# Attention weights of a pair turned by one transfer instead of two, with a new plan of loads and units

## The chip, the cores and the metric

The kernel runs on one core of a Trainium2 chip. The metric is the device time of one execution in microseconds (us). Engines are named as the profile names them: PE multiplies matrices (PEld is its weight load), DVE, ACT and POOL work on vectors, SP issues transfers (DMA). PE and its products write to banks of an accumulator memory; the other data lie in a memory of 128 partitions.

## The reference

Two stages follow each other. The first is attention with a decay, over 8 batches of 8 heads, 576 positions and 64 numbers per head:

```
scores = q @ k^T / 8 + cum[:, None] - cum[None, :]     # cum: running sum of log(clip(f)) of this head
scores = -1e9 where key > query                        # causal
attn   = softmax(scores); x = attn @ v
```

The second takes the 4608 rows of x (8 heads x 64 = 512 numbers each) through a gated block: g = x @ w_gate, out = (g * sigmoid(g) * (x @ w_val)) @ w_out, with 1536 inner columns. All inputs and the output are float32.

## The kernel before, in words

**Units.** Two heads make a pair (32 pairs, p = 0 to 31, four to a batch). The 576 queries of a head are cut in 9 blocks of 64, and a block of both heads of a pair fills 128 partitions. The blocks come in two groups: group 0 has blocks 0 to 3, group 1 blocks 4 to 8 (HI and LO, lines 224 and 225). A unit is a pair and a group.

**One pair.** k and q are loaded (load_pair, L385), cast to bf16 (prepare, L410 to L414), turned on PE into a bank named tx (L428) and copied out as kt and qz (L440, L442); qz takes two copies, one for each head. The running sums of log f of all heads are made once at the start (L342 to L345), written to DRAM (L354) and loaded per pair as cb, spread over partitions (L394); pair 0 gets its cb through a product with a matrix of ones instead (select, L369, and copies L373). scores makes products q by k into banks named sp, of which there are two (L461, and L465 for the causal mask), DVE adds cb and keeps the row's extreme (L477: t, tm), ACT takes the exponential with the row's sum (L491: e or eo). normalize adds a guard to the sums and inverts them (L505 to L509: lr), then POOL, or ACT for pairs under 8, scales e to bf16 weights (L526, L524) in a buffer pk, in slices of 128 keys by 128 queries: 6 slices for group 0, 19 for group 1 (NSL, line 226).

**Turning the weights.** The product with v needs the slices with keys on partitions. For pairs 0 to 7 (ON_PE, line 230) PE turns each slice with the identity matrix (L550) into a bank, and DVE or ACT copies it to a buffer pT (L555). For pairs 8 to 31 a transposing transfer on SP's queue writes pT from pk (L538), one for each group. There are two pk and two pT buffers for each group. weighted multiplies pT by v (L576, into a tx bank, 4 products for group 0 and 10 for group 1), spread copies the result into xT (L600), a ring of 2560 columns. BOTH (line 237) is the pair from which the two groups are weighted in one operation of 14 products; below it each group has its own.

**The second stage.** The rows go in tiles of 256, 256, seven of 512, 256, 128 and 128 (TILES). gate makes the products with w_gate and w_val (L657, both into banks gv, from x of all four pairs of the batches in question), ACT takes tanh (L663), two DVE operations make hh (L665, L668); project multiplies by w_out (L685), halves (L692, L694) and stores (L696). The weights are loaded by POOL's queue in column blocks with a cast (L632, L636): wg0 and wv0 are columns 0 to 255, wg2 and wv2 256 to 511, and so on. v is loaded in five pieces for a batch (L615) and cast (L619).

**What sets the order.** The code writes no order for the engines by hand. Every step is an Op with its engines and an estimated length, reads, writes, a priority and, for transfers, a wire time. Plan.order (from L59) is a list scheduler: again and again it takes the operation that can start first by these estimates (ties by priority), gives it an engine and a buffer, and so fixes each engine's order; the engines then run in that order and wait on semaphores. SPARE is a handicap, in ns, for ACT and DVE on casts and scalings; MOST bounds how many gv banks turned weights (p), output (o) and gate products (f) may hold; SOON, BACK and CBACK say how early loads of a pair may go; SLACK bears on which line of a shared pool goes first. STARTUP (line 244) is the order of the first loads: p is k and q of a pair, f9 the log f input, c a pair's cb, v a piece of v, w a block of weights. A load waits until the one AHEAD places ahead of it has landed, a weight load on POOL also for the one BEHIND places ahead. HEAD (line 245) is the order of the first eight units: group 0 of pairs 0 to 3, then group 1 of pairs 1, 0, 3, 2.

The functions that the diff touches:

Of the kernel before, what the change touches and what calls it, by code (L numbers as in the profile page):

```python
# [9 lines left out]
BF16 = mybir.dt.bfloat16  # L10
# [21 lines left out]
class Plan:  # L32
# [6 lines left out]
    def __init__(self):  # L39
        self.slack = 0  # L40
        self.ops, self.pools, self.home, self.where, self.turn, self.banks = [], {}, {}, {}, {}, set()
        self.line, self.most = {}, {}

    def pool(self, name, bufs):
        self.pools[name] = bufs

    def key(self, key, pool, turn=None, line=None):

        self.home[key], self.turn[key], self.line[key] = pool, turn, line

    def buf(self, key):
        return self.pools[self.home[key]][self.where[key]]
# [6 lines left out]
    def order(self):  # L59
        writers, users = {}, {}  # L60
        for o in self.ops:
            for k in o.writes:
                writers.setdefault(k, []).append(o)
            for k in {*o.writes, *o.reads, *o.holds}:
                users.setdefault(k, []).append(o)
        waiting, kids = {}, {}
        for o in self.ops:
            deps = {d.n: d for k in o.reads for d in writers[k] if d is not o}
            deps.update((d.n, d) for d in o.after)
            o.deps = list(deps.values())  # L70
# [12 lines left out]
        lines = {}  # L83
        for name, x in turn:
            lines.setdefault(name, []).append((name, x))
        left = {k: len(v) for k, v in users.items()}
        until = {k: 0 for k in users}
        slots = {name: [None] * len(b) for name, b in self.pools.items()}
        free = {e: 700 for e in ("PE", "DVE", "ACT", "POOL", "SP")}
        wire = {True: 0, False: 0}  # L90
        ready = {o.n: 0 for o in self.ops if not waiting[o.n]}
        done, using = [], {}

        def room(o, now=None):

            at, take = 0, []
            for k in o.writes:
                if k not in self.home or k in self.where:
                    continue
                name, best = self.home[k], None  # L100
                x = name, self.line[k]
                mine = sum(x == (self.home[y], self.line[y]) for y, _ in take)
                if turn[x][taken[x] + mine] != k:
                    return None
                if x in self.most:
                    held = sum(y is not None and left[y] > 0 and self.line[y] == x[1] for y in slots[name])
                    if held + mine >= self.most[x]:
                        return None
                for n, held in enumerate(slots[name]):
                    if any(n == b and name == self.home[x] for x, b in take):  # L110
                        continue
                    t = 0 if held is None else until[held] if not left[held] else None
                    if t is not None and (best is None or t < best[0]):
                        best = (t, n)
                if best is None:
                    return None
                at = max(at, best[0])
                take.append((k, best[1]))
            if now is not None:
                for k, _ in take:  # L120
                    for x in lines[self.home[k]]:
                        if x[1] != self.line[k] and taken[x] < len(turn[x]):
                            y = turn[x][taken[x]]
                            q = opener[y]
                            if rank(y) < rank(k) and q.n in ready and ready[q.n] <= max(now, at) + self.slack and room(q) is not None:
                                return None
            return at, take

        while ready:
            best = None  # L130
            for n, r in ready.items():
                o = self.ops[n]
                got = room(o, r)
                if got is None:
                    continue
                for e, dur in o.engs.items():
                    s = max(r, got[0], free[e])
                    for k in o.reads:
                        if k in using and using[k][0] != e:
                            s = max(s, using[k][1])  # L140
                    c = (s + o.bias.get(e, 0), o.prio, n, e, dur, got[1])
                    if best is None or c[:4] < best[:4]:
                        best = c
            if best is None:
                raise RuntimeError("no operation can start: " + ", ".join(str(self.ops[n].writes) for n in list(ready)[:20]))
            s, _, n, e, dur, take = best
            o = self.ops[n]
            s -= o.bias.get(e, 0)
            if e == "PE" and s < COLD:
                dur *= 2  # L150
            for k, b in take:
                name = self.home[k]
                self.where[k] = b
                slots[name][b] = k
                taken[name, self.line[k]] += 1
            o.start, o.eng = s, e
            free[e] = s + dur
            for k in o.reads:
                if self.home.get(k) in self.banks:
                    using[k] = e, s + dur + 30  # L160
            if o.dma:
                q = e == "POOL"
                at = max(wire[q], s + (2550 if q else 2000))
                both = max(0, min(2 * o.dma, wire[not q] - at))
                wire[q] = at + o.dma + both / 2
                wire[not q] += both / 2
                if o.ring:
                    free[e] = max(free[e], wire[q] - 1450)
                o.end = wire[q] + 1100
            else:  # L170
                o.end = free[e] + o.lat
            for k in {*o.writes, *o.reads, *o.holds}:
                left[k] -= 1
                until[k] = max(until[k], o.end)
            del ready[n]
            for kid in kids.get(n, ()):
                waiting[kid.n] -= 1
                if not waiting[kid.n]:
# [12 lines left out]
def kernel(  # L191
# [305 lines left out]
    def normalize(p, g):  # L497
# [10 lines left out]
        pl.op({"DVE": 95, "ACT": 200}, guard, [("ls", p, g)] + ([("z", "ls", n) for n in range(6)] if p < 3 else []), [("lr", p, g)], s, lat=120)  # L508
        pl.op({"DVE": 95}, lambda e: nc.vector.reciprocal(lr(), lr()), [("lr", p, g)], [("l2", p, g)], s, lat=170, holds=[("lr", p, g)])  # L509
        kk = ("pk", p, g)  # L510
        pl.key(kk, f"pk{g}")
        w = HI[g] - LO[g] + 1
        for i in range(HI[g], LO[g] - 1, -1):
            m = i // 2 + 1
# [18 lines left out]
                      [kk], s, lat=100)  # L533
                o.bias = SPARE
        tk = ("pT", p, g)
        pl.key(tk, f"pT{g}")
        if (p, g) not in ON_PE:
            pl.op({"SP": 300 + 153 * NSL[g]}, lambda e: nc.sync.dma_start_transpose(  # L538
                out=pl.buf(tk), in_=pl.buf(kk).rearrange("p s k -> p (s k)")),
# [202 lines left out]
    for o, (a, z) in evacs:  # L742
        for lo, hi, t in spans:
            if lo < z - NRING and a - NRING < hi:
                o.after.append(gates_of[t])

    with tc.manual_schedule():
        for o in pl.order():
            o.fn(o.eng)
# [30 lines left out]
```

## Time and profile before

| | us |
|---|---|
| median of 3 runs (lowest to highest) | 423.09 (422.11 to 423.39) |
| the profiled execution | 422.81 |
| its span | 420.9 |
| busy: PE / DVE / ACT / POOL | 401.0 / 338.2 / 301.8 / 255.2 |
| start of the first PE product / of the first gate product | 4.9 / 35.1 |
| last weighted product (pair 31) | 350.6 |
| transposing transfers | 48, from 101.7 to 345.9 |
| moved by DMA | 72.22 MB, mean 172 GB/s |

The span runs from the first to the last profiled instruction; the execution's time has 1.9 us more around it. PE's busy time is the union of its products' spans as the profile models them: products are pipelined, so a full row of nines says that something is always in flight, not that PE works at its peak. A wait is the idle time of an engine ahead of an instruction, put down to what came last. SP moves nothing itself; its issue of a transfer is not counted as busy, and the transfer lands later.

### The profile page before, as it was taken

The numbers are of one execution on the slowest core, as the hardware profiler recorded it, in microseconds if no ns is written. First come the engines' busy times: TensorE is split into PE (matmuls) and PEld (weight loads), VectorE is DVE, ScalarE is ACT, GpSimd is POOL, SyncE is SP. The second block draws the span as 40 slices with busy tenths as digits, with TensorE's granted clock in tenths as the row PEclk, the third lists the DMA queues.
The fourth block names the chain that finished last, engine by engine and source line by source line (L and its number), as shares of the span: only waits on it lengthen the run. The fifth ranks groups of instructions, "written<-read, shape, count | busy, mean of one in ns | idle before, by whom it ended". The sixth has DMA issues, their size and how long they took to land.

```text
span 420.9 us, 10065 instructions
## 1 busy us (share of the span) xinstructions
PE 401.0 (95%) x3304; PEld 233.1 (55%) x3304; DVE 338.2 (80%) x1072; ACT 301.8 (72%) x848; POOL 255.2 (61%) x461
## 2 busy tenths in 40 slices
PE   3679999999999999999999999999999999999996
PEld 1546787765545545554555555555544544457675
DVE  4689899999998979988898899799978962765233
ACT  4689799999998857987777777877885953332221
POOL 8679968979977782987288478757776350000000
PEclk9999999999999999999999999999999999999999
DMA  6999997997999799999999998899889184000211
GB/s 175 201 171 212 238 230 166 205 233 183 191 228 200 191 203 188 223 179 207 209 212 225 220 208 187 212 209 211 198 203 235 21 165 92 0 26 25 76 51 51
DMA packets 143796, 72.22 MB, mean 172 GB/s; under 512 B 118528, under 2 KB 130560, under 8 KB 143744
## 3 DMA queue, kind: packets, MB, share of 16 engines
q1 hardware_dynamic: 137572, 66.28, 74.9%
q0 software_dynamic: 5808, 4.72, 7.7%
q10 hardware_dynamic: 364, 0.59, 0.5%
q8 instruction: 26, 0.43, 0.4%
q14 instruction: 26, 0.21, 0.2%
HBM read 47.04 MB, written 9.58 MB: 135 GB/s over the span
## 4 chain that ended last, share of the span: by engine, by line
PE 80%; POOL 5%; ACT 5%; DVE 3%; issue 2%; POOLq 0%; DVEq 0%; ACTq 0%
PE gv L657 39%; PE gv L685 21%; PE sp L461 9%; PE tx L576 6%; POOL pk L526 3%; PE tx L428 3%; PE gv L550 2%; DVE t L477 2%; PE sp L465 2%; ACT e L491 2%; ACT eo L491 1%; POOL kb L414 1%; POOL qb L412 1%; ACT th L663 1%; ACT pT L555 0%
## 5 line engine op out<-in xcount | busy, mean ns | idle before, releaser
L477 DVE CUSTOM_DVE_ANT_0 t<-sp,cb 128x512 f32<-128x512 f32 (+7 forms) x288 | 129.6, 474 | 11.1 <-PE sp L465 5.9
L526 POOL TENSOR_SCALAR pk<-e,lr 128x512 bf16<-128x512 f32 (+3 forms) x189 | 99.9, 532 | 52.6 <-DVE lr L509 20.8
L657 PE MATMUL gv<-xT,wv 128*128 128x512 bf16 (+2 forms) x576 | 111.3, 326 | 0.0
L657 PE MATMUL gv<-xT,wg 128*128 128x512 bf16 (+2 forms) x576 | 111.3, 326 | 0.0
L685 PE MATMUL gv<-wo,hh 128*128 128x512 bf16 (+1 forms) x444 | 105.6, 373 | 0.0
L665 DVE SCALAR_TENSOR_TENSOR th<-th,gv 128x512 f32<-128x512 f32 x108 | 73.8, 684 | 35.6 <-ACT th L663 34.7
L663 ACT ACTIVATE th<-gv 128x512 f32<-128x512 f32 x108 | 63.9, 592 | 50.3 <-PE gv L657 49.9
L491 ACT ACTIVATE e<-t,tm 128x448 f32<-128x448 f32 (+4 forms) x160 | 88.4, 554 | 13.7 <-DVE tm L477 13.2
L668 DVE TENSOR_TENSOR hh<-th,gv 128x512 bf16<-128x512 f32 x108 | 73.8, 683 | 5.3 <-PE gv L657 1.3
L461 PE MATMUL sp<-kt,qz 128*128 128x448 bf16 (+4 forms) x320 | 73.1, 298 | 3.5 <-DVE tm L477 3.2
L491 ACT ACTIVATE eo<-t,tm 128x256 f32<-128x256 f32 (+3 forms) x128 | 70.7, 553 | 2.2 <-DVE tm L477 1.9
L526 POOL TENSOR_SCALAR pk<-eo,lr 128x384 bf16<-128x384 f32 (+3 forms) x127 | 67.4, 531 | 2.8 <-DVE lr L509 2.5
L657 PEld LDWEIGHTS <-wv 128*128 128x128 bf16 x576 | 49.5, 98 | 35.1
L657 PEld LDWEIGHTS <-wg 128*128 128x128 bf16 x576 | 49.2, 98 | 34.9
L685 PEld LDWEIGHTS <-hh 128*128 128x128 bf16 x444 | 39.7, 98 | 38.3
L465 PE MATMUL sp<-mask,ident 128*128 128x64 bf16 x288 | 48.1, 198 | 0.0
L461 PEld LDWEIGHTS <-qz 128*128 128x128 bf16 x320 | 31.1, 102 | 20.7 <-issue 1.9
L412 POOL TENSOR_SCALAR qb<-qf 72x1024 bf16<-72x1024 f32 x32 | 33.3, 1041 | 9.5 <-DMA qf<-in_q_dram 8.6
L465 PEld LDWEIGHTS <-ident 128*128 128x128 bf16 x288 | 27.2, 100 | 15.2 <-issue 4.2
L692 ACT ACTIVATE ot<-gv 128x512 f32<-128x512 f32 (+1 forms) x24 | 14.1, 586 | 27.6 <-PE gv L685 27.6
L619 POOL CAST vt<-vf 128x512 bf16<-128x512 f32 (+1 forms) x40 | 24.0, 608 | 13.4 <-DMA vf<-in_v_dram 13.3
L414 POOL CAST kb<-kf 96x768 bf16<-96x768 f32 x31 | 26.0, 839 | 9.9 <-DMA kf<-in_k_dram 8.8
(58 smaller groups left out, 395.1 us busy)
## 6 DMA issues: line engine op xcount, KB each, us to landing
out_dram<-ot SPq DMA_DIRECT2D x35, 256.0 KB
kf<-in_k_dram SPq DMA_DIRECT2D x31, 288.0 KB
qf<-in_q_dram SPq DMA_DIRECT2D x31, 288.0 KB
cb<-cum_f SPq DMA_DIRECT2D x62, 144.0 KB
vf<-in_v_dram SPq DMA_DIRECT2D x32, 256.0 KB
wo<-in_moe_w_out_dram POOLq DMA_DIRECT2D x3, 512.0 KB, 10.0
vf<-in_v_dram SPq DMA_DIRECT2D x8, 128.0 KB
wv<-in_moe_w_val_dram POOLq DMA_DIRECT2D x2, 512.0 KB, 9.1
```

Source lines behind the costliest of these rows:

```text
L412: eng[e].tensor_scalar(dst, src, -scale, 1.0, op0=ALU.mult, op1=ALU.mult)
L414: eng[e].tensor_copy(dst, src)
L461: nc.tensor.matmul(sp[:, o:o + z - a], qz[:, i, :, :].rearrange("p h r -> p (h r)"), kt[:, a:z], start=True, stop=not last)
L465: nc.tensor.matmul(sp[:, o - QB:o], ident, mask, start=False, stop=True)
L477: nc.vector.tensor_tensor_reduce(out=pl.buf(tk)[:, a:z], in0=pl.buf(sk)[:, o:o + z - a], in1=pl.buf(("cb", p))[:, a:z], scale=1.0, scalar= ...
L491: nc.scalar.activation(pl.buf(ek)[:, :L], pl.buf(tk)[:, :L], AF.Exp, bias=pl.buf(("tm", p, g))[:, i:i + 1], scale=-1.0, accum_out=pl.buf(( ...
L526: eng[e].tensor_scalar(dst, src, r, 1.0, op0=ALU.mult, op1=ALU.mult)
L657: nc.tensor.matmul(pl.buf(bk)[:, j * n:j * n + n], wt[:, ko, fc * P:fc * P + P], xT[:, ko, x0:x0 + n], start=ko == 0, stop=ko == KD - 1)
L663: pl.op({"ACT": 487}, lambda e, u=u: nc.scalar.activation(pl.buf(("th", t, u)), pl.buf(("wg", t, u)), AF.Tanh, scale=0.5), [("wg", t, u)], ...
L665: pl.op({"DVE": 605}, lambda e, u=u: nc.vector.scalar_tensor_tensor(pl.buf(("th", t, u)), pl.buf(("th", t, u)), 1.0, pl.buf(("wg", t, u)), ...
L668: pl.op({"DVE": 605}, lambda e, u=u: nc.vector.tensor_mul(pl.buf(("hh", t, u)), pl.buf(("th", t, u)), pl.buf(("wv", t, u))), [("u", t, u), ...
L685: nc.tensor.matmul(pl.buf(bk)[:, 0:z - a], hh[:, (fc % nf) * n + ms * P:(fc % nf) * n + ms * P + P], wo[:, fc, a:z], start=fc == 0, stop=f ...
```

## The change

It has four parts. First, pk and pT of both groups become two views of one buffer of 25 slices (two such buffers each), the group 1 slices in front. For pairs 8 to 31 both groups must take the same of the two buffers (the argument same of Plan.key, the test twin in Plan.order), and group 0 issues one transfer that reads all of pk and writes all of pT, after both groups are scaled. Second, scores of both groups of a pair are recorded ahead of both normalizations, group 1's normalization first. Third, the planner's numbers and the first loads' order change, BOTH goes from 6 to 8. Fourth, two tables are new: NUDGE adds to the priority of all operations of a unit, and WAIT adds to the handicap of one; unit() names the unit of an operation (a is the softmax side of a pair and group, q the preparation of k and q, v the v of a batch, f the gate of a tile, o its projection).

```
-        self.line, self.most = {}, {}
+        self.line, self.most, self.same = {}, {}, {}
...
+        if same is not None:
+            self.same[key] = same
...
+                twin = self.where.get(self.same.get(k))
                 for n, held in enumerate(slots[name]):
+                    if twin is not None and n != twin:
+                        continue
...
-    MOST = (("p", 2), ("o", 2), ("f", 3))
-    AHEAD = 7
-    BEHIND = 6
-    BOTH = 6
-    SPARE = {"ACT": 500, "DVE": 900}
+    MOST = (("p", 1), ("o", 2), ("f", 3))
+    AHEAD = 10
+    BEHIND = 8
+    BOTH = 8
+    SPARE = {"ACT": 400, "DVE": 700}
...
-    SLACK = 2500
-    SOON = 6
+    SLACK = 0
+    SOON = 4
...
-    STARTUP = "p0 f9 f0 p1 c1 p2 p3 c2 v00 c3 wv0 wg0 wg2 wv2 v04 v01 wv4 v03 c4 v02 wg4 p4 wg8 wv8 p5 v10 wo0 p6 c5 c6 v14 wo4 v11 v13 v12 p7 c7 wo8"
+    STARTUP = "p0 f9 p1 c1 p2 p3 c2 c3 v00 v04 f0 wg0 wv2 wv0 wg4 wv4 v02 v01 wg2 p4 wv8 v03 wg8 v10 c4 p6 p5 c5 wo8 p7 wo0 v14 v11 v12 c7 c6 wo4 v13"
...
+    NUDGE = "a5.0:1 a5.1:-1 a9.1:1 a10.1:2.5 a11.1:1.5 a12.0:1.5 a14.0:1.5 a15.0:2 a19.1:-2 a22.0:3 a23.0:1 a25.0:-1.5 a26.0:0.5 a27.1:1 f3:-8.5 f5:5 f7:1 f8:9.5 o0:1 o4:-2 o5:-3.5 o6:-2 q0:2 q4:-2 q20:-0.5 q31:-1 v0:-8"
...
+    WAIT = "a2.0:100"
...
-    for g in range(2):
-        bufs(f"pk{g}", [P, NSL[g], P], BF16, 2)
-        bufs(f"pT{g}", [P, NSL[g], P], BF16, 2)
+    both = {}
+    for n in ("pk", "pT"):
+        both[n] = [sb.tile([P, sum(NSL), P], BF16, name=f"{n}{x}") for x in range(2)]
+        pl.pool(n + "1", [x[:, 0:NSL[1], :] for x in both[n]])
+        pl.pool(n + "0", [x[:, NSL[1]:, :] for x in both[n]])
...
-        pl.key(kk, f"pk{g}")
+        joint = not any((p, x) in ON_PE for x in range(2))
+        pl.key(kk, f"pk{g}", same=("pk", p, 1 - g) if joint else None)
...
-        pl.key(tk, f"pT{g}")
+        pl.key(tk, f"pT{g}", same=("pT", p, 1 - g) if joint else None)
+        if joint:
+            if g == 0:
+                pl.op({"SP": 300 + 153 * sum(NSL)}, lambda e: nc.sync.dma_start_transpose(
+                    out=both["pT"][pl.where[tk]], in_=both["pk"][pl.where[kk]].rearrange("p s k -> p (s k)")),
+                    [kk, ("pk", p, 1)], [tk, ("pT", p, 1)], s - 1, dma=500 + 118 * sum(NSL)).ring = True
+            return
...
             scores(p, g)
+        for g in (1, 0):
             normalize(p, g)
...
+    nudge, leave = ({k: float(v) for k, v in (y.split(":") for y in x.split())} for x in (NUDGE, WAIT))
+    for o in pl.ops:
+        u = unit(o)
+        if u is not None and o not in line:
+            o.prio += nudge.get(u, 0)
+            o.bias = {e: o.bias.get(e, 0) + leave.get(u, 0) for e in o.engs}
```

More of the change, by code (lines that the diff above doesn't have):

```diff
@@ L41, in __init__, with key @@
         self.ops, self.pools, self.home, self.where, self.turn, self.banks = [], {}, {}, {}, {}, set()
-        self.line, self.most = {}, {}
+        self.line, self.most, self.same = {}, {}, {}
     def pool(self, name, bufs):
         self.pools[name] = bufs
-    def key(self, key, pool, turn=None, line=None):
+    def key(self, key, pool, turn=None, line=None, same=None):
         self.home[key], self.turn[key], self.line[key] = pool, turn, line
+        if same is not None:
+            self.same[key] = same
     def buf(self, key):
@@ L745, with unit @@
                 o.after.append(gates_of[t])
+    def unit(o):
+        w = o.writes[0] if isinstance(o.writes[0], tuple) else (o.writes[0],)
+        n, *i = w[0] + w[1:] if isinstance(w[0], tuple) else w
+        if n in ("kb", "qb", "kt", "qz", "cm", "kf", "qf", "cb") or n == "tt" and isinstance(i[0], str):
+            return f"q{i[0] if n != 'tt' else i[1]}"
+        if n in ("sp", "lr", "l2", "pk", "pT", "tt", "xo"):
+            return f"a{i[0]}.{i[1]}"
+        if n in ("t", "e"):
+            return f"a{i[0]}.{int(i[1] > HI[0])}"
+        if n == "x":
+            return f"a{i[1] // NB * NPB + i[0]}.{int(i[1] % NB > HI[0])}"
+        if n in ("vf", "vt"):
+            return f"v{i[0]}"
+        if n in ("wg", "wv", "th", "u", "hh") and len(i) == 2:
+            return f"f{i[0]}"
+        return f"o{i[0]}" if n in ("op", "ot", "out") else None
+    nudge, leave = ({k: float(v) for k, v in (y.split(":") for y in x.split())} for x in (NUDGE, WAIT))
[4 more added lines that the diff above has]
+            o.bias = {e: o.bias.get(e, 0) + leave.get(u, 0) for e in o.engs}
     with tc.manual_schedule():
```

## The prediction, as it was put on record

> **What bounds the kernel now.** I read the page's busy shares and its forty slices first, then the busy time of each engine by stretch, then who waits for whom with PE as the waiter, then the timeline of DVE and PE up to 36 us, and last the source line of the transposing transfers.
>
> The page says that PE is busy for 401.0 of 420.9 us, and at the full granted clock (1.00 in every stretch).
>
> ```profile
> PE   3679999999999999999999999999999999999996
> DVE  4689899999998979988898899799978962765233
> DMA  6999997997999799999999998899889184000211
> ```
>
> The stretches (columns: stretch, its length, then busy us and instructions of PE, PEld, DVE, ACT and POOL, the clock, the DMA share, GB/s) put the 19.9 us in which PE is idle in their places:
>
> ```profile
> 0.00:35.00 35.00, 20.84 (x162) 13.76 (x163) 23.80 (x90) 24.87 (x75) 27.00 (x66) 1.00 0.94 183
> 40.00:60.00 20.00, 19.03 (x237) 15.37 (x236) 17.71 (x50) 16.48 (x39) 16.27 (x24) 1.00 1.12 241
> 60.00:80.00 20.00, 18.90 (x216) 15.25 (x215) 19.55 (x68) 18.61 (x52) 17.09 (x30) 1.00 0.88 185
> 120.00:340.00 220.00, 219.92 (x1690) 114.48 (x1689) 196.31 (x655) 174.32 (x521) 149.43 (x263) 1.00 0.99 197
> ```
>
> 14.2 us lie in the first 35, 2.07 between 40 and 80, 0.34 between 100 and 120, 0.08 between 120 and 340, 3.24 after the last product (5.90 less 2.66 in the stretch from 415 us). So from 80 us on PE sets the pace and nothing but less PE work, or a new wait, can move the end; the change leaves PE's 3304 products as they are. What can be won lies in the start, and a little between 40 and 110 us.
>
> Who ends PE's waits up to 36 us (us in total, times, longest):
>
> ```profile
> PE sp L461 <- DVE tm L477: 3.2, 7, 1.2
> PE gv L369 <- DVE t L345: 2.3, 1, 2.3
> PE tx L428 <- POOL qb L412: 2.0, 1, 2.0
> ```
>
> No row has PE waiting for pT, the output of the transfers that the change joins. Before 80 us these are not transfers at all: pairs 0 to 7 are turned on PE in both kernels.
>
> **The start, walked.** In the changed program's order PE turns k of pair 1 first and k of pair 0 later; pair 0's k is cast by DVE, its q by ACT, and q of pair 3 by ACT. The rows of before that carry the walk:
>
> ```profile
> 6.45 1.35 DVE L345 TENSOR_TENSOR_SCAN t<-tiny,t 64x576 f32<-64x576 f32 x1
> 13.51 0.42 DVE L477 CUSTOM_DVE_ANT_0 t<-sp,cb 128x256 f32<-128x256 f32 x1 [1.44 <-PE sp L465]
> 16.75 1.52 DVE L442 COPY qz<-tx 64x576 bf16<-64x576 bf16 x2 [1.50 <-PE tx L428]
> 23.07 0.42 DVE L477 CUSTOM_DVE_ANT_0 t<-sp,cb 128x256 f32<-128x256 f32 x1 [0.74 <-ACT eo L491]
> ```
>
> (1) k of pair 1 is cast by POOL until 8.42, so its turning ends at 8.85, and the select products (L369), which ran from 7.95 to 10.20 (2.25 us), run from 8.85 to 11.1: 0.9 later. (2) ACT then copies q of pair 1 (2 x 0.64) ahead of pair 0's (2 x 0.64) instead of pair 0's alone: from 11.75 they end at 14.3, so the first score comes at about 14.4 where it came at 12.57: 1.8 later. (3) This is covered. DVE idled 1.44 and 1.50 us there, since everything after pair 0 waited for q of pair 2, cast by POOL from 14.88 when its load landed. That load starts when pair 0's q buffer is free, which is 8.97 (ACT's cast) instead of 9.44, so q of pair 2 comes at the same time or up to 0.5 earlier, and DVE's two copies of it start near 16.7 as before. Were the cover gone, the 1.8 us would be paid in full. (4) ACT casts q of pair 3 ahead of pair 0's exponentials and waits for that load. Issued at about 9.75 instead of 10.48, and with the 5.41 us that q of pair 2 took from issue to its cast (9.47 to 14.88), it lands at 15.2; the cast (bounds 0.84, a k cast on ACT, and 1.06, POOL's q cast; taken as 1.05) ends at 16.25, the four exponentials (1.76) at 18.0. The row sums come back in time for DVE at 18.3, as before. (5) From there DVE is the engine to follow. One of the two copies of q of pair 3 goes to ACT (0.76 less on DVE), two 0.1 us sums come in, and the wait of 0.74 at 23.07 has time to go: pair 3's first group is added by 23.4 to 23.8 instead of 24.79, about 1.0 earlier.
>
> (6) The first gate product needs tile 0 of x, whose last copy is DVE's; it came at 35.1. In the new order DVE does the rest of pair 3 and three adds of pair 2 ahead of that copy: adds of 512 columns 0.62, of 448 0.55, 384 0.50, 320 0.45, 64 0.22, copies of turned weights 0.5 to 0.68. From "pair 3 added" to that copy I count 13.9 us of DVE work, so the gate starts at 37.3, or 37.9 with the 0.6 us of small waits that this stretch showed: 2.6 to 2.8 later. But PE does more ahead of it: nineteen turnings of pair 1 (56 ns apart, 1.06) and five score banks (1.0). PE's loss up to the gate is thus 2.7 less 2.1: **+0.6 us**, with ends at -1.0 (DVE's wait of (5) gone and no small waits) and +2.5 (the cover of (3) gone).
>
> **Between 40 and 110 us.** PE's idle 2.41 us there, and slow starts of scores behind DVE, come from POOL, ACT and DVE being nearly full at once (DVE 19.55 of 20). In the new order the adds of pairs 2 and 3 are done some 4 us earlier against the gates, the k and q of pair 4 are cast together ahead of pair 3's second group, and the scores of pair 4 stand 4 us of PE work earlier (the products ahead of them in the order, each by its spacing in the trace). What was idle can go at most; the starts of PE's products in the timeline show about as much again hidden in "busy" (a product of 64 columns that starts 0.3 to 0.5 us after the one ahead of it where 29 ns is its spacing elsewhere). I take **-2.5 us**, between -5 (all of it) and +2 (as much again, when an in-order engine meets a different load time). Two pairs (6 and 7) are weighted in two products instead of one: 14 products took 0.88 us together, 10 alone 0.71 (40.67 to 41.38), and 4 alone some 0.3 from the x8 of two groups in 0.82: **+0.2** each or less, +0.3 taken for both.
>
> **The joint transfer.** 48 transfers become 24, one of 25 slices (19 + 6).
>
> ```profile
> L538 SPq DMA_TRANSPOSE pT<-pk x48: 1210/2202/5728, 101.7 to 345.9; - x48
> ```
>
> The columns are shortest, median and longest issue on SP in ns. Six slices take 1.21 to 1.56 us, nineteen 2.85 to 5.73: at best 0.127 us a slice and 0.45 fixed, so SP gives up 24 x 0.45 = 10.8 us of issue time. By the row above PE does not wait for it: **0**. It costs lateness instead. Group 1's slices used to go while POOL still scaled group 0; now all 25 start when group 0 is ready, and land 2.4 us later than group 0's six at best (19 x 0.127), up to 4.5 later (5.73 less 1.21). From the end of group 0's issue to the weighted products I find 3.5 us (pair 31) to 17 (pair 8), under 5 in 14 of 24 pairs. The new order puts scores of pairs 15 to 31 earlier by up to 17 us of PE work, counted in the same way, which covers it in part. Behind the waiting transfer in SP's queue stand loads of k, q, cb, v and the stores.
>
> The Trainium skill ("DMA: Bandwidth & Descriptors", Queues, rings and completion order) says that an engine takes a ring's descriptors in order, which speaks against the change: loads of later pairs stand behind a longer piece. By that rule alone the sum would move toward the case "late transfers" below. Its section "Rules for kernel authors" says to coalesce small transfers into one large; by that rule the sum would move toward "relief". The trace has both directions in the issue times and decides neither.
>
> **Sum.** +0.6 - 2.5 + 0.3 + 0 = -1.6; the range of edits from the walk alone is -5.7 to +4.8. I round the gain up to 2.3 us, nearer to the -5 end of the second term, since its rows show two full engines being unloaded at that place. Against the profiled execution's 422.81 us (span 420.9 and 1.9 around it; 0.28 under the median of 423.09) that is 420.5 us. This measurement can tell some 0.3%, 1.3 us, from no change.
>
> **The rivals.**
> - *Terms cancel* (0.22): the start loses what the middle wins, 422 to 424. For: the walk's two terms have opposite signs and like size.
> - *Late transfers, slower* (0.17): the weighted products, in order on PE, wait for the joint transfer. It decides where less than about 5 us lie between group 0's last scaling and the product. Half of 14 pairs' margin lost, 0.4 us each at the middle of 2.4 to 4.5, is 6 us: 427, and up to 432. Against: no such wait now, and scores run further ahead.
> - *Crowded first loads, slower* (0.10): the first gate weights are issued near 11.5 us instead of 17.83, among the q and cb loads, while DMA is at 0.82 and soon over 1.0; q of pair 2 lands 2 us later, the cover of (3) is gone and the +2.5 end plus 1 for the late wg of the second column block comes: 424.1 to 427.
> - *Relief, faster* (0.06): if the fixed parts of the transfers hold back loads in the 0.99 busy DMA stretch, their 10.8 us come back: 412. Against: PE idles only 0.08 us there.
> - That the change does not do what it says is excluded: the new program holds 24 transfers of 25 slices.
>
> My forecast holds 0.45 (417.5 to 421.5). Faster 0.45 + 0.06 = 0.51, same 0.22, slower 0.27. The range leaves out most of "relief" and the upper half of "late transfers": 415 to 428. The forecast's own range is 417.5 to 421.5.
>
> **What would show it.** First score near 14.4 and first gate near 37.9 us; DVE without a wait at 16.75 to 24; PE over 19.4 us busy in both stretches from 40 to 80; transfers of 3.6 us or more on SP; no row of PE waiting at L576's line. Wrong if PE waits for pT, if the first gate comes before 36 or after 40, or if PE's idle time between 40 and 110 grows.

## The result, and the profile after

| | before | after |
|---|---|---|
| median (lowest to highest), runs | 422.6 (421.01 to 423.39), 4 | 426.62 (425.73 to 428.95), 4 |
| ratio (95% interval) | | 1.0114 (1.0081 to 1.0147) |
| the profiled execution; its span | 422.81; 420.9 | 427.18; 425.4 |
| first PE product / first score / first gate product | 4.94 / 12.57 / 35.1 | 8.48 / 15.29 / 40.17 |
| transposing transfers, sum of their issue times on SP | 48, 122.0 us | 24, 113.1 us |

The kernel after is 1.1% slower, some 4 us. The forecast was 420.5 and faster, so it was wrong in sign, though 426.6 lies in its range. Among the experiments below one run each of b_joint_free, b_free and b_joint_kq was in a slower state (434.58, 525.58 and 443.36 us): their medians hold it, their ratios leave it out.

The same rows of the page, after:

```profile
PE   2679979999999999999999999999999999999996
DVE  5688949999999999949897799879779851685232
DMA  6999999599999999799999999999984441000211
```

PE has one new digit under 9, the sixth (53 to 64 us, a 7), and starts lower. Four of the stretches of after (length, busy us and instructions of PE, PEld, DVE, ACT, POOL, clock, DMA share, GB/s):

```profile
0.00:35.00 35.00, 20.22 (x143) 13.21 (x144) 24.54 (x94) 25.13 (x72) 25.93 (x66) 1.00 0.95 191
40.00:60.00 20.00, 17.12 (x194) 13.79 (x193) 14.07 (x38) 14.20 (x30) 16.41 (x25) 0.91 1.15 209
60.00:80.00 20.00, 20.00 (x233) 17.12 (x231) 18.90 (x63) 18.68 (x52) 12.75 (x22) 1.00 1.01 216
120.00:340.00 220.00, 218.34 (x1700) 113.69 (x1697) 190.59 (x654) 183.17 (x543) 156.77 (x277) 1.00 0.98 201
```

From 60 to 80 us PE is now busy throughout (18.90 before): that gain came. Against it stand 2.88 us idle between 40 and 60 with a granted clock of 0.91, 0.6 less work by 35 us, and 1.66 us idle between 120 and 340 (0.08 before).

The clock column hides one thing. The trace's first record of the clock lies at 33.08 us in before and at 37.86 in after, and the time ahead of it counts as 1.00. But PE's turnings of 128 columns follow each other every 106 to 107 ns up to 31.3 us in before and 37.8 in after, and every 56 ns from 36.2 and 38.0 on. So PE ran at half its later rate for the first 33 and 38 us, and after stays in that state some 5 us longer.

Three rows of who ends PE's waits, after (us in total, times, longest):

```profile
PE tx L441 <- POOL kb L427: 8.7, 2, 8.5
PE gv L677 <- DMA wg<-in_moe_w_gate_dram: 2.9, 1, 2.9
PE tx L596 <- DMA pT<-pk: 0.7, 1, 0.7
```

The first row is the start: PE has nothing until POOL's cast of k of pair 1 ends at 8.42. The second is the idle time that begins at 52.5 us, while PE waits for a block of w_gate. The third is a wait for a joint transfer, at 242.02. Three rows of the start on DVE, after:

```profile
16.09 0.42 DVE L490 CUSTOM_DVE_ANT_0 t<-sp,cb 128x256 f32<-128x256 f32 x1 [0.83 <-PE sp L478]
17.08 1.52 DVE L455 COPY qz<-tx 64x576 bf16<-64x576 bf16 x2
22.90 0.42 DVE L490 CUSTOM_DVE_ANT_0 t<-sp,cb 128x256 f32<-128x256 f32 x1
```

The scores come 2.6 to 2.7 us later (16.09 against 13.51 for the first add), and the copies of q of pair 2 only 0.33 later, without a wait: the cover that the walk relied on was there. The wait of 0.74 us ahead of the add at 23.07 is gone (22.90). The joint transfers on SP (shortest, median, longest issue in ns):

```profile
L553 SPq DMA_TRANSPOSE pT<-pk x24: 3725/4582/6580, 106.5 to 341.3; - x24
```

**Where the 4.5 us of span went.** I added up, over PE's 3304 products, by how much each started later than its usual spacing behind the one ahead. Up to 40 us PE lost 25.1 us before and 28.0 after (+2.9); from 40 to 80, 7.3 and 7.3; from 80 to 120, 4.3 and 4.2; from 120 to 360, 21.7 and 23.3 (+1.6). Together +4.4. The even 40 to 80 us hides two things of opposite sign. The wait for w_gate with the slow clock behind it costs some 4.4 us: the first product behind the wait starts 3.0 us late, and eight gate and ten weighted products take 1.82 and 1.16 us from their first start to the next product's, where two such groups in before (49.67 and 50.63) took 0.96 and 0.64. The rest of the stretch got about as much better.

### The profile page after: what moved, and what is told of

The parts are those of the page before. It is cut to its first block, busy times and chain, and to the rows that moved or that the text cites. A ratio compares the mean times of both kernels' runs of the same rounds, so it can differ in the third digit from the quotient of the medians.

```text
span 425.4 us, 9975 instructions
## 1 busy us (share of the span) xinstructions
PE 402.7 (95%) x3304; PEld 233.6 (55%) x3304; DVE 330.5 (78%) x1056; ACT 308.3 (72%) x862; POOL 255.0 (60%) x463
## 4 chain that ended last, share of the span: by engine, by line
PE 74%; DMA 12%; DVE 5%; ACT 4%; POOL 2%; issue 2%; SPq 1%; DVEq 0%; POOLq 0%; ACTq 0%
PE gv L677 37%; PE gv L705 19%; PE sp L474 7%; PE tx L596 5%; DMA wg<-in_moe_w_gate_dram 4%; DMA kf<-in_k_dram 4%; PE tx L441 3%; DVE t L490 3%; DMA qf<-in_q_dram 2%; DMA pT<-pk 2%; PE sp L478 1%; PE gv L570 1%; ACT e L504 1%; ACT eo L504 1%; DMA out_dram<-ot 1%
## 5 line engine op out<-in xcount | busy, mean ns | idle before, releaser
L490 DVE CUSTOM_DVE_ANT_0 t<-sp,cb 128x320 f32<-128x320 f32 (+7 forms) x288 | 130.9, 475 | 12.7 <-PE sp L478 6.5
L540 POOL TENSOR_SCALAR pk<-e,lr 128x512 bf16<-128x512 f32 (+1 forms) x192 | 101.4, 532 | 50.4 <-DVE lr L522 15.7
L474 PE MATMUL sp<-kt,qz 128*128 128x448 bf16 (+5 forms) x320 | 75.4, 303 | 4.6 <-DVE tm L490 3.2
L504 ACT ACTIVATE eo<-t,tm 128x384 f32<-128x384 f32 (+3 forms) x128 | 71.0, 555 | 4.5 <-DVE tm L490 3.9
L478 PE MATMUL sp<-mask,ident 128*128 128x64 bf16 x288 | 49.3, 200 | 0.0
L425 POOL TENSOR_SCALAR qb<-qf 72x1024 bf16<-72x1024 f32 x30 | 31.2, 1040 | 9.7 <-DMA qf<-in_q_dram 7.1
L712 ACT ACTIVATE ot<-gv 128x512 f32<-128x512 f32 (+1 forms) x26 | 15.2, 585 | 29.9 <-PE gv L705 29.9
L427 POOL CAST kb<-kf 96x768 bf16<-96x768 f32 x31 | 25.5, 826 | 14.4 <-DMA kf<-in_k_dram 13.1
L453 ACT COPY qz<-tx 64x576 bf16<-64x576 bf16 x42 | 26.4, 630 | 5.9 <-PE tx L441 5.4
```

What stands on the lines that cost most here:

```text
L425: eng[e].tensor_scalar(dst, src, -scale, 1.0, op0=ALU.mult, op1=ALU.mult)
L453: nc.scalar.copy(dst, src)
L474: nc.tensor.matmul(sp[:, o:o + z - a], qz[:, i, :, :].rearrange("p h r -> p (h r)"), kt[:, a:z], start=True, stop=not last)
L478: nc.tensor.matmul(sp[:, o - QB:o], ident, mask, start=False, stop=True)
L490: nc.vector.tensor_tensor_reduce(out=pl.buf(tk)[:, a:z], in0=pl.buf(sk)[:, o:o + z - a], in1=pl.buf(("cb", p))[:, a:z], scale=1.0, scalar= ...
L504: nc.scalar.activation(pl.buf(ek)[:, :L], pl.buf(tk)[:, :L], AF.Exp, bias=pl.buf(("tm", p, g))[:, i:i + 1], scale=-1.0, accum_out=pl.buf(( ...
```

## The experiments

Each run stands beside runs of the kernel before on the same chip; ratios are to those. "Frozen" kernels keep the order of before or of after and change only what the edit says.

**1. Joint transfer and plan, each alone.** In the order of before, group 1's transfer is dropped and group 0's place holds the joint one (b_joint). In the code of after, the planner's numbers and the first loads' order are put back, without NUDGE and WAIT (p_joint_alone), or only the joint transfer is taken out (p_not_joint); the planner orders both anew. p_joint_alone keeps the second part of the change too, the scores of both groups recorded ahead of both normalizations.

```
 b_joint         order of before; group 0: dma_start_transpose(both["pT"], both["pk"]); group 1: none
 p_joint_alone   STARTUP, MOST, AHEAD, BEHIND, BOTH, SPARE, SLACK, SOON of before; NUDGE = WAIT = ""
 p_not_joint     joint = False
```

> The kernel before with its order frozen and joint buffers; group 1's transfer is left out and group 0's place takes one of 25 slices. Nothing else is moved. Theory L: PE had 3.5 to 17 us between group 0's transfer and the weighted product, and a joint one lands some 2.4 us later than six slices; 422 to 424 us, within 0.3% of the kernel before. Rival J: 425 to 428, with PE waiting at the weighted products.

> The changed kernel's code with the numbers and the first loads' order of before and empty NUDGE and WAIT tables: the joint transfer alone, planned anew. Its order up to the first gate is that of before. Theory L' (first loads and start cost most; a joint transfer costs only where the order leaves it no time): 422 to 424.5 us, less than the 425.3 of the joint transfer in the frozen old order, since the planner knows its length. Rival J' (a joint transfer is late in any order): 425 or more, with PE waiting for pT.

> The changed kernel with separate transfers, planned anew with all of the change's numbers, first loads and nudges. The order up to the first gate is that of the changed kernel. Theory L': the late gate and the wait for wg8 are in it, 425 to 429 us. Rival J': without the joint transfer the time of before comes back, 421 to 423.

| | separate transfers | joint transfer |
|---|---|---|
| order of before, frozen | 421.74 | 425.29, 1.0090 (1.0073 to 1.0107) |
| numbers and loads of before, planned | 421.35 | 426.65, 1.0120 (1.0096 to 1.0145) |
| numbers, loads and nudges of after, planned | 445.94, 1.0563 (1.0529 to 1.0597) | 426.62, 1.0114 (1.0081 to 1.0147) |

The joint transfer by itself costs 3.6 us in the frozen order; planned anew, together with the new order of recording, it costs 5.3. The new numbers don't win it back: with the joint transfer, both plans take the same time. They fit the joint transfer only; with two transfers they cost 24.6 us. So the two parts can't be priced apart from each other; taken in this order, first the joint transfer and then the plan, the whole loss comes with the first (with the new recording in it). Both joint kernels show the wait that the forecast priced at nothing. PE's waits in b_joint (us in total, times, longest):

```profile
PE tx L578 <- DMA pT<-pk: 2.1, 3, 1.2
```

and in p_joint_alone:

```profile
PE tx L596 <- DMA pT<-pk: 4.8, 6, 1.4
```

Before has no such row.

**2. Parts of the new plan.** Two transfers in the frozen order of after (a_two_transfers); the loads of before with all else of after (p_old_loads); no nudges (p_no_nudge); the steps to the first gate, and one piece of v with them, put back by 16 moves (a_early_gate).

```
 a_two_transfers  order of after; both transfers, 19 and 6 slices, where the joint one stood
 p_old_loads      STARTUP, AHEAD = 7, BEHIND = 6 of before
 p_no_nudge       NUDGE = WAIT = ""
 a_early_gate     order of after; 16 operations of pairs 0 to 3, of the first gate and of v moved
```

> The changed kernel with its order frozen; in the place of each joint transfer of 25 slices SP issues two, 19 slices and then 6. Theory L: the joint transfer is not the cause, 426 to 428 us, if anything a little slower for 24 more issues on SP. Rival J: the weighted products come sooner, 422 to 424.

> The changed kernel, but with the first loads' order, AHEAD and BEHIND of before, planned anew. Theory L': the waits for wg8 or w_out on PE between 50 and 85 us go or shrink to under 1 us, 422 to 425 us. Rival (loads late by any order, as DMA is full until 100 us): another load is late, 426 or more.

> The changed kernel with empty NUDGE and WAIT tables, planned anew. Theory L': start and first loads as in the changed kernel, so 425 to 429 us. Rival (the nudges themselves bring the loss): 421 to 424.

> The changed kernel with its order frozen, except for the steps to the first gate product: the turning, copying and weighting of group 0 of pairs 0 to 3, the copies into x, the first gate product and the piece 1 of v are put where the kernel before has them relative to the scores of pair 3. The late wg8 stays. Theory L: first gate near 36.5 instead of 40.2 us, PE's loss in the first 40 us smaller by 2 to 3 us, but part of it is lost again in a longer wait for wg8, which lands at 55.4 whatever PE has done: 425 to 427 us, with the wait for wg8 at 4 to 6 us. Rival (the two losses add up): 423 to 424.5 and the wait unchanged.

Measured, in this order: 435.14, 1.0325 (1.0290 to 1.0359); 432.01, 1.0254 (1.0225 to 1.0284); 430.61, 1.0213 (1.0187 to 1.0239); 429.82, 1.0192 (1.0177 to 1.0206). Every part put back alone makes the kernel after slower: by the ratios the nudges are worth 4 us, the loads' order 6 and the joint transfer 9 in that order. p_old_loads has no wait of PE for w_gate or w_out left, as its theory asked, and is slower than after all the same; its turnings come 56 ns apart only from 48 us on. An earlier first gate alone wins nothing: a_early_gate has it at 36.31 instead of 40.17 and waits as long for w_gate (2.9 us), then more for scores (4.4 us, 3.2 in after) and pT (2.7, 0.7 in after).

**3. The late load of w_gate.** In after, POOL issues w_val's last third ahead of w_gate's:

```profile
36.91 0.80 POOL L652 DMA_DIRECT2D wv<-in_moe_w_val_dram  x1
39.40 0.79 POOL L652 DMA_DIRECT2D wg<-in_moe_w_gate_dram  x1
```

The second lands at 55.38, 15.98 us after its issue (in before it went at 37.62 and took 11.74), and PE, which is there at 52.5, waits. Four single microseconds (columns as above):

```profile
54.00:55.00 1.00, 0.00 (x0) 0.00 (x0) 0.01 (x2) 0.00 (x0) 0.99 (x2) 0.96 1.12 181
55.00:56.00 1.00, 0.57 (x3) 0.44 (x4) 0.00 (x0) 0.00 (x0) 1.00 (x2) 0.50 1.24 209
57.00:58.00 1.00, 1.00 (x8) 0.54 (x8) 0.00 (x0) 0.65 (x2) 1.00 (x2) 0.50 1.33 239
59.00:60.00 1.00, 1.00 (x19) 0.97 (x17) 1.00 (x5) 0.94 (x1) 0.00 (x0) 1.00 1.19 216
```

After the idle 2.9 us the granted clock is 0.50 until 58, and eight gate products of 256 columns take 1.89 us of busy time instead of 1.03. Four kernels take the wait away: by swapping the two loads (a_wg8_first), by also issuing the third load of w_out behind its second (a_wg8_wo4), and, with every load in its place, by letting the first block's gate products read the first third of w_gate where they would read its last, so that this use is left out (a_wg8_free), with pT's waits taken out as well (a_both_free).

```
 a_wg8_first   order of after; load wg8 ahead of wv8
 a_wg8_wo4     the same, load wo4 right behind wo0
 a_wg8_free    if t == 0 and wt is wg: fc = fc % 8
 a_both_free   the same, and for p >= 8 weighted reads w_val in place of pT
```

> The changed kernel with its order frozen; alone, POOL issues the load of the third column block of w_gate (wg8) just ahead of that of w_val (wv8) instead of after it. Theory L (loads and start): PE's wait of 2.9 us for wg8 at 55 us goes, and with it the stretch at half the granted clock behind it (about 1.5 us in the profiled execution); wv8 then lands near 55.4, ahead of its first use, so nothing takes the wait's place: 422.5 to 424 us, 3 to 4 less than the changed kernel. Rival J (the joint transfer costs the time): no change, 426 to 427, since DVE and the transfers hold the later work back anyway. Rival N: the wait moves to wv8, 425 to 426.

> The order of the kernel after, with the load of the last third of w_gate put ahead of that of w_val (which moved the wait to w_out) and the third load of w_out issued right behind its second. Theory (after loses 2.9 us and a stretch at half the clock to one late load, and whichever load is last takes the wait on): both waits go, and the time is 422.5 to 424.5, 2 to 4 us below after. Rival (the loads share one rate, so that another one, of k, q or v, takes the wait): 426 to 428.5, with a new wait between 55 and 110 us.

> The kernel after, with the gate products of the first block of tokens reading the first third of w_gate where they read its last: every load is still made at its place, and PE doesn't wait for the late one (2.9 us and a stretch at half the clock). The output of that block isn't the reference's. Theory (the late load is worth its wait and the slower clock): 3 to 4 us below after's ratio of 1.0114, so 1.002 to 1.005. Rival (the work behind is bound by another chain, so the wait taken out comes back before 120 us): 1.008 to 1.012.

> The run before it, with the weighted products of pairs 8 to 31 reading a fixed stretch of w_val too, so that neither the late load nor a joint transfer is waited for. Theory: 0.7 to 1.6 us below that run, 0.998 to 1.003; what stays over 1 is the start, where PE had lost 2.9 us more than in before. Rival (the joint transfer costs after as much as it cost in the order of before): 3 us or more below that run.

Measured: 427.98, 1.0135 (1.0109 to 1.0161); 425.2, 1.0113 (1.0084 to 1.0143); 426.56, 1.0117 (1.0085 to 1.0148); 427.64, 1.0127 (1.0097 to 1.0157). None is below after's 1.0114 by more than the intervals allow. In a_wg8_free the wait has moved to w_out (in a_wg8_first it is the same 2.4, in a_both_free 2.2):

```profile
PE gv L707 <- DMA wo<-in_moe_w_out_dram: 2.4, 1, 2.4
```

So in three of the four the wait moves on, as the rivals had it: the loads share the DMA (share 1.15 and 1.01 in the stretches from 40 to 80 us), and PE, freed of one late load, arrives early at the next. a_wg8_wo4 has neither wait:

```profile
40.00:60.00 20.00, 19.95 (x252) 17.16 (x251) 17.59 (x47) 18.43 (x44) 16.96 (x26) 1.00 1.13 209
60.00:80.00 20.00, 19.84 (x223) 15.95 (x225) 19.76 (x67) 18.51 (x50) 16.29 (x29) 1.00 1.05 215
```

and its profiled execution is the shortest of this order (span 421.4). Yet its six runs are 423.3, 423.79, 424.04, 426.36, 426.48 and 426.81, and the runs of before beside it 420.19: no gain that the ratio shows. What its three longer runs lose isn't known; the profile is of a short one.

a_both_free answers one more question: it takes the waits for pT out of after, and that wins nothing either. By the same addition as above PE loses some 1.5 us less than in after between 40 and 80 us and some 3 us more between 120 and 360. There it waits for k and q, 3.4 us in three waits (1.0 in two in after). The longest is for a k whose load stood on SP behind two joint transfers, begun at 227.37 and 235.42:

```profile
235.42 4.31 SPq L553 DMA_TRANSPOSE pT<-pk  x1
242.07 0.54 SPq L398 DMA_DIRECT2D kf<-in_k_dram  x1
249.20 0.43 PE L441 MATMUL tx<-ident,kb 96*128 96x96 bf16 x6 [1.60 <-POOL kb L427]
```

After issues the same transfers and loads in the same places and waits 0.3 us there, for the same k. No run moves these loads in the order of after.

**4. Is it lateness?** First test: 51 blocks of gate or project products are put ahead of the weighted products in the order of before, with the joint transfer and with two; a_all does it to a_wg8_wo4.

```
 b_joint_later  51 blocks (gate, project) of L659 and L687 ahead of L578 of pairs 8 to 31
 b_later        the same in before
 a_all          a_wg8_wo4 and 56 such blocks
```

> The order of the kernel before with the joint transfer, which alone took 425.29 us against 421.74 beside it; here each of pairs 8 to 31 also has one to three blocks of gate or project products (51 in all, each block about 0.9 us start to start) put ahead of its weighted product on PE instead of behind it. Theory (the joint transfer lands late): the three waits of PE for pT (2.1 us in the profile) go, 120 to 360 us loses 21 to 22.5 us instead of 25.7, and the time is 421.5 to 423. Rival (the joint transfer costs by what it does to other transfers or by its own length, not by PE waiting for it): 424.5 to 426, with waits for other loads as before. Second rival (what the weighted product feeds is due at once): the waits move to the attention output's turns and to the projections behind it, 424 to 427.

> The control of the run before it: the kernel before, with its two separate transfers, and the same 51 blocks put ahead of the weighted products. Nothing waits for pT in the kernel before, so by the theory nothing is to be won: 421.5 to 422.5, the ratio within 0.3% of 1. If the moved blocks win something by themselves (rival), the time is under 420.5, and what the run with the joint transfer wins isn't lateness; if they cost, it is over 423.

> The run before it with 56 blocks of gate or project products put ahead of the weighted products of pairs 8 to 31 as well. Theory: the pT waits of after are small (0.7 us in one, 1.6 us with the ones for q and k), so this is worth 1 to 2 us on top: 421 to 423.5, about the kernel before. Rival: the same as the run before it, within 0.7 us.

Measured: 448.07, 1.0654 (1.0625 to 1.0684); 448.06, 1.0642 (1.0617 to 1.0667); 451.22, 1.0719 (1.0688 to 1.0751). All my numbers were wrong by 25 us or more. In b_joint_later the wait for pT falls to 0.4 us, but PE now waits for DVE at the scores, which stand behind the moved blocks:

```profile
PE sp L463 <- DVE tm L479: 15.5, 34, 1.2
```

(3.3 us, 8 times, in b_joint.) Moving the blocks lengthened another chain of the kernel, so this proves little; with the weighted products this late, joint and separate transfers take the same time.

Second test, without moving anything: for pairs 8 to 31 the weighted products read a stretch of w_val that has long been loaded; all transfers are still made. The kernel leaves out the use of the turned weights, so no transfer waits for a pT buffer to be read either.

```
                     for h in range(2):
+                        if p >= 8:
+                            pT, a = wv[:, 0, :].rearrange("p (s k) -> p s k", k=P), min(a, KF - n)
```

> The order of before with the joint transfer (b_joint, 425.29 us beside 421.74, ratio 1.009), but the weighted products of pairs 8 to 31 read a fixed stretch of w_val, long loaded, where they read pT: the transfers are all still made, and no product of these pairs waits for one. What is left out is the use of the weights, so the output isn't the reference's. Theory (PE waits for the joint transfer's landing): the cost goes, the ratio to before is 0.998 to 1.003. Rival (it costs by the queue, by other transfers or by what DVE and ACT lose): the ratio stays at 1.006 to 1.010.

> The control: before with its two separate transfers, its weighted products of pairs 8 to 31 reading the same fixed stretch of w_val. Before shows no wait for pT, so nothing should be won: the ratio is 0.997 to 1.002. If it is under 0.995, waits for pT too short to show cost before as well, and b_joint_free must be read against this one.

Measured: 424.51, 1.0055 (1.0035 to 1.0076), and 421.83, 1.0008 (0.9993 to 1.0023). The control is clean: before pays nothing for pT that shows. With the joint transfer the direct waits are about 1.5 of the 3.6 us (1.0090 less 1.0055, by the intervals 0.4 to 2.6), and some 2 us stay. The timeline shows one place for them. SP and the turning of one q in b_free:

```profile
262.64 1.34 SPq L538 DMA_TRANSPOSE pT<-pk  x1
264.04 0.58 SPq L385 DMA_DIRECT2D kf<-in_k_dram  x1
264.67 0.41 SPq L385 DMA_DIRECT2D qf<-in_q_dram  x1
272.11 0.42 PE L428 MATMUL tx<-ident,qb 72*128 72x72 bf16 x8
```

and in b_joint_free, with POOL's cast of that q:

```profile
262.91 3.93 SPq L540 DMA_TRANSPOSE pT<-pk  x1
266.88 0.58 SPq L387 DMA_DIRECT2D kf<-in_k_dram  x1
267.51 0.42 SPq L387 DMA_DIRECT2D qf<-in_q_dram  x1
272.17 1.04 POOL L414 TENSOR_SCALAR qb<-qf 72x1024 bf16<-72x1024 f32 x1 [0.99 <-DMA qf<-in_q_dram]
273.26 0.43 PE L430 MATMUL tx<-ident,qb 72*128 72x72 bf16 x8 [0.74 <-POOL qb L414]
```

The transfer starts at the same time, but keeps SP 3.93 us instead of 1.34; the loads behind it leave 2.84 us later, POOL casts q later (268.69 in b_free), and PE waits. In this order the k and q of 17 pairs stand right behind a joint transfer, or a step or two further. The last two runs put these loads ahead of it.

```
 b_joint_kq       b_joint; 34 loads (kf, qf) moved from behind the joint transfer to right ahead of it
 b_joint_kq_free  the same, reading w_val in place of pT
```

> The order of before with the joint transfer (ratio 1.009), and the k and q loads of 17 pairs that stood on SP right behind a joint transfer issued right ahead of it. Theory (the cost is in two parts: PE waits for the landing, and loads queue on SP behind a transfer that is 3 us longer): the second part, some 2 us, goes, and the ratio is 1.002 to 1.006, with no wait of PE for q's casts after 120 us. Rival (the loads find the transfer's lateness instead, since SP issues them first, or the cost is elsewhere): 1.007 to 1.011.

> The same, with the weighted products of pairs 8 to 31 reading a fixed stretch of w_val, so that PE waits for no joint transfer either (the use of the weights is left out). Theory: both parts gone, the ratio is 0.998 to 1.002, beside 1.0055 for the run with the loads behind the transfer. Rival (what was left is neither, for instance POOL waiting 8 us for weights that the transfer reads late): 1.004 to 1.007.

Measured: 436.92, 1.0359 (1.0329 to 1.0388), and 423.64, 1.0036 (1.0018 to 1.0054). The first was to be faster and is 11 us slower. Its waits:

```profile
PE tx L578 <- DMA pT<-pk: 11.9, 9, 3.0
```

SP issues the loads first, here in b_joint_kq (the weighted product behind this transfer starts at 150.44, after a wait of 3.0 us):

```profile
141.08 0.44 SPq L387 DMA_DIRECT2D kf<-in_k_dram  x1
141.57 0.44 SPq L387 DMA_DIRECT2D qf<-in_q_dram  x1
142.18 5.54 SPq L540 DMA_TRANSPOSE pT<-pk  x1
```

and in b_joint (the product starts at 148.29, after a wait of 1.2 us):

```profile
140.73 3.87 SPq L540 DMA_TRANSPOSE pT<-pk  x1
144.66 0.58 SPq L387 DMA_DIRECT2D kf<-in_k_dram  x1
```

The transfer goes 1.45 us later and its issue takes 1.67 us longer, with the loads under way beside it, so it ends 3.1 us later. Taking the use of pT away (b_joint_kq_free) brings the time down by 13.3 us, about the 11.9 of waits. This settles that in the order of b_joint_kq a late joint transfer sets the end. Whether the queue behind it is the rest is less sure: 1.0055 falls to 1.0036, with overlapping intervals, and some 1.2 us over b_free's 1.0008 stay open. POOL's waits for pk, which the joint transfer reads late (3.1 us once in b_joint_kq_free, 8.2 in b_joint_free, none in b_free), are a candidate that wasn't tried alone.

## Why the prediction was wrong

**The step that failed** is the joint transfer, priced at 0 "by the row above PE does not wait for it". Measured alone it costs 3.6 us (b_joint), enough to turn the sum from -1.6 to +2. The row spoke of two transfers, of which the one that starts last has 6 slices, not of one with 25. The working had what was needed: 2.4 to 4.5 us later landing, and under 5 us of room in 13 of 24 pairs (it says 14). In b_joint, the products that wait started 5.9 to 7.6 us after the joint transfer's issue; in before, the weighted products start 4.7 to 17.6 us after group 0's issue, under 5.87 in nine of 24 pairs, short by 4.3 us in sum. That sum was there to be made and gives the sign. That it lies near the 3.6 is partly luck, since the direct waits for pT are only some 1.5 to 2.1 us of it and the rest came in other ways, in part through the loads behind the transfer on SP. The rival "late transfers" named the mechanism and its condition; its 6 us was too large; one reason, argued and not measured, is that the room which a late product leaves serves the next. In after itself PE's waits for pT are 0.7 us, and no run shows how much of after's own 4 us the joint transfer is.

The Trainium skill ("DMA: Bandwidth & Descriptors", Rules for kernel authors) would coalesce many small transfers into one large one; here the 9 us of issue time saved on SP (10.8 forecast) bought nothing. Its section Queues, rings and completion order, where descriptors are taken in ring order, pointed the right way: the trace shows SP's issue in order, 2.84 us for the loads behind; no run here separates the ring from that.

**The start, +0.6.** It cost +2.9. Steps (1) and (3) came as walked, and (5) nearly: the cast ended at 8.42, the copies began at 17.08 against "near 16.7", pair 3's first group was added at 24.05 against 24.79 (forecast 23.4 to 23.8). The first score came at 15.29 instead of 14.4: the two pairs of copies of q stand 0.69 us apart on ACT, an idle time that before had too and that step (2) left out. The first gate came at 40.17 instead of 37.9. The stretch of DVE work from 24.05 to there:

```profile
24.05:40.17 16.12, 14.08 (x96) 7.71 (x95) 14.10 (x54) 13.39 (x42) 15.07 (x29) 1.00 1.04 194
```

DVE was busy for 14.10 us of it, against 13.9 counted, and its adds took as long as in before (0.69 us for 512 columns). It idled 2.0 us, where the walk allowed 0.6 for small waits; the longest waits were for scores from PE (0.50 and 0.27 us, at 31.77 and 33.16). So DVE's work was counted rightly and the waits were too small. The walk also took the clock as full and put PE's turnings 56 ns apart, which they reached in after at 38 us. The slower products cost PE about as much in both kernels up to 40 us (5.7 us before, 5.4 after, against their later spacings); whether they delayed after's scores and gate is not tested. The bound of +2.5 was meant for a lost cover, and the loss passed it with the cover in place. a_early_gate put the gate earlier and didn't gain by it.

**40 to 110 us, -2.5.** The gain came (60 to 80 us is full), about 4.4 us by starts against usual spacing. It was taken back in the same stretch by one load: 2.9 us of wait and 1.4 by the half clock behind it. I had one late wg in a rival for 1 us; it was the third block, and its landing took 15.98 us. Section 3 shows that this wait isn't worth its length, since the next load takes it on.

**Separately weighted pairs, +0.3,** were not measured alone. **120 to 340 us** was said to have nothing to lose but by a new wait: +1.6. PE's waits there are 0.7 (q, 171.19), 0.7 (pT, 242.02) and 0.3 us (k, 247.95). After's plan leaves at least 6.8 us between issue and product where before's leaves 4.7; that goes with its few waits for pT.

**The sum** was -1.6 and was "rounded up" to -2.3 by leaning to the favourable end; the measured terms are +2.9, 0 and +1.6. All three signs of being wrong came: PE waits for pT, the first gate comes after 40, and PE's idle time between 40 and 110 us grew from 2.41 to 2.93.

What stays open: why no removal of the load waits shows in the median of after, though the waits for k and q in a_both_free point at the loads behind the joint transfers; and some 1.2 us of the joint transfer's cost in the order of before.

## What to carry to other kernels

A merged transfer starts when its last part is ready and lands later by the length of the rest: before pricing it at nothing, list for each use the time from the issue of the last part to the waiting instruction, and sum what falls short. Count also what is queued behind it on the issuing engine; here 9 us of saved issue time won nothing. A row without waits tells of the old arrangement. A wait that is taken away alone may only move to the next load: test it before you count it as won.

## What the runs showed of the hardware

PE's first products ran at half the later rate, and the full rate came at 33.1 us in before, 37.9 in after and between 28 and 48 us in the other runs that have a record of it. A PE idle time of 2.88 us was followed by about 3 us at a granted clock of 0.50 (55 to 58 us), and one of 2.4 us in a_wg8_first likewise (0.50 from 80 to 83 us), so that a late load cost some 1.4 us more than its wait in after and 1.7 in a_wg8_first (by starts against usual spacing). The Trainium skill ("TensorE: Matmul & The Clock Gate", Part 1: The HAM clock gate) gives half rate after an idle window of about 3.4 us; here waits shorter than that were enough. Weight loads of 512 KB with a cast took from 5.8 us (issued at 23.29) to 16.0 us (39.40) from issue to landing in after; the two longest, 13.3 and 16.0, were issued within 2.5 us of each other, and the DMA share from 40 to 60 us was 1.15. The 256 KB block of w_gate issued at 31.52 took 5.0 us.
